# First mixing layer of a two-layer FNet and GeGLU kernel: hidden-side products of the last 1024 rows as seven turned block products

## The chip, the cores and the metric

One NeuronCore of a Trainium2 chip runs the whole program. The metric is device time in microseconds (us) of one execution. Engines are called as the profile calls them: PE is TensorE, DVE VectorE, ACT ScalarE, POOL GpSimd, SP SyncE, which issues most loads. Each engine works through its own list of instructions in the order in which the list was written when the program was built; a helper (`schedule_with_timeline_sim`) fixes these lists at build time.

## The reference

The input x has 2048 rows of 512. Two kinds of layer alternate, and the pair is applied twice (layers 0 to 3 in the kernel):

```python
def _A_ref(x, dft_seq_re, dft_seq_im, dft_hid_re, dft_hid_im):
    a = jnp.einsum("bsd,ed->bse", x, dft_hid_re)
    b = jnp.einsum("bsd,ed->bse", x, dft_hid_im)
    y = jnp.einsum("ts,bse->bte", dft_seq_re, a) - jnp.einsum("ts,bse->bte", dft_seq_im, b)
    return y
def _B_ref(x, w_gate, w_up, w_down):
    return (_gelu(x @ w_gate) * (x @ w_up)) @ w_down
x = x + _A_ref(_layernorm(x, axis=-1), ...)
x = x + _B_ref(_layernorm(x, axis=-1), ...)
```

## The kernel before

**Precision.** Each fp32 operand is divided into two fp32r parts, hi and lo (`split`: ACT writes hi at L157, DVE writes lo = src - hi at L159). Each product is three matmuls of 128x512, hi by hi, hi by lo, lo by hi (`mm3`, L214 to L216).

**A mixing layer** (`mix`, layers 0 and 2) forms the sequence-side product first, for four blocks b = 0 to 3 of 512 output rows, then multiplies its two results (real m = 0, imaginary m = 1) by the hidden-side matrices `wh`. The sequence side of a block is a 2x2 block product done with seven products (Winograd's form): A11 and A12 products, made for all four blocks at the beginning of the layer (`FORE`), then the stage "S2" (products S2, S1, S3 in a skewed order; for each of 8 pieces three DVE sums, `make_s2`, and three splits) and the stage "S4" (products S4 and A22). So S2 has 144 matmuls and S4 has 96. At the end of S4, DVE reads the PSUM banks (`plus`, L194) to finish the four columns pieces `cs[m, c]` of the block.

**The hidden side** of a block is done in one of two ways.

- Plain (`hid_groups`): eight pieces (m, c), each split and multiplied on four row tiles: 8 x 4 x 3 = 96 matmuls, in the order of `EARLY_HID` (2 pieces, between S2 and S4), `MID_HID` (4) and `LATE_HID` (2). The rows of x are put into the PSUM banks first (`seed`, L208), and ACT copies the finished banks out (`x_out`, L201).
- Paired (`pair_groups`, with `PAIRED = {2: (2, 3)}`: layer 2, blocks 2 and 3 together): the 1024 rows are again a 2x2 block product in seven products P1 to P7, each of 4 pieces k on 2 banks, 7 x 4 x 2 x 3 = 168 matmuls. The result comes out turned (columns on partitions), so that DVE transposes it in 32x32 blocks and adds it to x (`turned_into`, L815 and L197), and x is loaded and stored in that form (`pair_wide_load`, `pair_out`). DVE also makes differences of the pieces (`arrived`, `pair_sums`). In the first block of a pair P1 and P2 are used (2 pieces early, 6 late), in the second P7 and P4 (2 early, 6 late); P6, P5 and P3 (`PAIR_REST`, 12 products of 6 matmuls) run beside the first window of the next layer through the list `spare` (`beside_mix`).

The paired form needs other pieces of the hidden-side weights: `whd[k]`, seven pieces for each of 4 values of k, made from `whc` by `weight_steps(k, whc, whd)`: three loads, four sums on half tiles, four splits, seven stores to DRAM on POOL's queue. They are made in layer 1, second window (w = 1), through `spare`.

**What sets the order.** `take` works ahead: up to 7 items (`AHEAD`) are loaded and split before they are used. Between hidden-side products jobs called chores are run, `-(-len(chores) // hid_left)` after each (`chores_at`): from block 1 on they are the norms, transposes, sums and splits of the next layer's first operand (`block_steps`), and in layer 0 two weights of that layer's up projection (`wgu`, from `weight_steps`). `down_pieces` puts the making of down-projection weights beside layer 0 as well.

**A feed-forward layer** (`geglu`, layers 1 and 3) has two windows w of 1024 rows and goes over 14 steps n in each. In layer 1, w = 0, it also makes the remaining weights, and it starts (`first(0)`) with a product whose bank is copied by ACT as seed of the next one (L208).

Of the kernel before, what the change touches and what calls it, by code (L numbers as in the profile page):

```python
# [53 lines left out]
def fnet_geglu(ctx: ExitStack, tc: tile.TileContext, x_in, ws, wh, wgu, wdn, wdc, whc, out):  # L54
# [410 lines left out]
    PAIR_REST = [(name, k) for name in ("P6", "P5", "P3") for k in (2, 3, 0, 1)]  # L465

    def pair_items(names):
        return [(F32R, (piece(whd[k], FORM[name]),), make_pair(name, k), (name, k)) for name, k in names]

    def skewed(n):  # L470

# [6 lines left out]
    def plan(layer):  # L478

        fore, steps = FORE[layer], []  # L480
        steps += [(b, "A11") for b in range(fore)] + [(b, "A12") for b in range(fore)]
        for b in range(NB):
            if b >= fore:
                steps += [(b, "A11"), (b, "A12")]
            if b in PAIRED.get(layer, ()):
                n = PAIRED[layer].index(b)
                steps += [(b, "S2"), (b, PAIR_EARLY[n]), (b, "S4"), (b, PAIR_LATE[n])]
            else:
                steps += [(b, "S2"), (b, EARLY_HID), (b, "S4"), (b, MID_HID), (b, LATE_HID)]
        return steps  # L490
# [23 lines left out]
    def mix_items(layer):  # L514
        def raw(make, *tiles):
            items.append((F32, tiles, make, None))

        for b, what in plan(layer):
            tiles = [[ws[(b * 2 + m) * NS + k] for k in range(NS)] for m in range(2)]
            (a11, a12), (a21, a22) = ((r[:NK], r[NK:]) for r in tiles)  # L520
            hold = b >= FORE[layer]
            if what == "A11":
                for k in range(NK):
                    raw(as_is if bare(layer, b, what, k) else make_a11(k) if hold else plain, a11[k])
            elif what == "A12":
                for k in range(NK):
                    raw(plain, a12[k])
            elif what == "S2":
                for i, k in skewed(3):
                    if layer and (b, k) in wss:  # L530
                        raw(plain, wss[b, k][i])
                    elif i == 0:
                        raw(make_s2(layer, b, k), a21[k], a22[k], *(() if hold else (a11[k],)))
                    else:
                        raw(make_s1(k) if i == 1 else make_s3(k))
            elif what == "S4":
                for i, k in skewed(2):
# [6 lines left out]
            elif b in PAIRED.get(layer, ()):  # L544
# [277 lines left out]
    def mix(layer):  # L822
        hid, sums, chores, hid_left = {}, {}, [], [0]

        def chores_at(b):
            if b == NB - 3:
                norms, others = block_steps(layer + 1, 0)
                later.update(norms=norms[NT:], fetches=others[:ND], others=others[ND:])
                return norms[:NT]
# [38 lines left out]
        xu, xv, pair_banks, kept_p, pair_wide, late_v, sums_due = {}, {}, {}, {}, {}, {}, []  # L868

        def arrived(b, m, c):  # L870
            if b not in paired:
                return
            t = cs.pop((m, c))
            if b == paired[0]:
                (xv if m else xu)[c] = t
                cs["P2" if m else "P1", c] = t
                return
# [20 lines left out]
        def pair_wide_load(n):  # L898
# [3 lines left out]
            moved(pair_wide[n], xs[layer, paired[n]], lambda v, rows: nc.sync.dma_start(v, rows))  # L902

        def pair_out(n):
            moved(pair_wide[n], xs[layer + 1, paired[n]], lambda v, rows: nc.gpsimd.dma_start(rows, v))

        LAST = {"P1": 3, "P2": 1, "P7": 3, "P4": 1, "P6": 1, "P5": 1, "P3": 1}
        FIRST = {"P1": 0, "P2": 2, "P7": 0, "P4": 2}
# [48 lines left out]
            pair_product(*PAIR_REST[i])  # L957

        def pair_groups(b, groups):
            n, early = paired.index(b), groups in PAIR_EARLY  # L960
            if early:
                chores.extend(chores_at(b))
                hid_left[0] = 16 if n else 8
                if not n:
                    fetch_sums(paired[1])
                pair_wide_load(n)
            for i, (name, k) in enumerate(groups):
                if not early and not n and i == 2:
                    s2_seeded(paired[1])
# [7 lines left out]
            if n and not early:  # L977
                pair_banks["P6"] = [ps8.get() for _ in range(2)]
                for c in range(2):
                    seed(pair_banks["P6"][c], kept_p["P1"][c])  # L980
                spare.extend(lambda i=i: pair_rest(i) for i in range(len(PAIR_REST)))

        def down_pieces(b, at):
            for _ in range(DOWN_RUNS[at][b]):
# [52 lines left out]
        def a12(b):  # L1037
            stream["more"] = 0
            if layer and b == 0:
                lend("x")  # L1040
                lend("z")
            side = side_banks.pop(b)
            for k in range(NK):
                six(side, "B21", k, False, k == NK - 1, "21" if b == NB - 1 else None)
# [14 lines left out]

        def s2(b):  # L1060
            last = b == NB - 1
            if b == 0:
                lend("z")
                lend("x")
            cs.update(cs_next)
# [36 lines left out]

        def s4(b):
            last = b == NB - 1
            if b == NB - 4:
                sb.reclaim("z")
            if paired and b == paired[0] - 1:
                sb.reclaim("x")
            one, three = sides.pop(b)
            u = us.pop(b)  # L1110
# [158 lines left out]
    def geglu(w, layer):  # L1269
# [517 lines left out]
```

## Time and profile before

| what | value |
|---|---|
| median of 3 runs | 1596.6 us (1596.59 to 1599.89) |
| span of the profiled execution | 1596.4 us |
| its instructions | 22835 |
| mean granted TensorE clock | 1.000 |
| bytes by DMA | 431.75 MB, mean 270 GB/s |
| chain that ended last, PE's share | 91% |

In the rows of groups, the columns are line, engine, operation, tiles written and read, shape and count, then after the bar busy time in us, mean ns of one instruction, and after the next bar the idle time ahead of them with what ended it. In the rows by stage the columns are the stretch in us, its length, and for each engine busy time and in brackets the number of instructions that touch the stretch, then the granted clock, the share of DMA time and GB/s. In the rows in order of time the columns are start in us, length in us, engine, line, operation, tiles, count, and in square brackets the idle time ahead with what ended it.

### The profile page before, as it was taken

Reading aid. Unit: us, or ns where it says so; the run is one execution under the profiler, and the core shown is the slowest. Engines: PE = TensorE matmul, PEld = TensorE weight load, DVE = VectorE, ACT = ScalarE, POOL = GpSimd, SP = SyncE. Lnnn points to the kernel's source line nnn. Section 1 sums busy time; section 2 is a strip of 40 time slices with the busy share of each in tenths; the row PEclk is TensorE's granted clock in tenths of the full one; section 3 lists DMA queues with packets and bytes.
Section 4 is the critical chain, followed back from the end, with each engine's and each line's share of the span. In section 5 each row is a group of like instructions: output and inputs, shape, how many; then the busy total and the mean of one; then the engine's idle time right before and its main releaser. Section 6 shows DMA issues by size and latency. Waiting matters only on the chain.

```text
span 1596.4 us, 22835 instructions
## 1 busy us (share of the span) xinstructions
PE 1590.0 (100%) x6984; PEld 1311.2 (82%) x6984; DVE 1169.2 (73%) x2030; ACT 891.6 (56%) x1731; POOL 294.9 (18%) x505
## 2 busy tenths in 40 slices
PE   9999999999999999999999999999999999999999
PEld 6888888888888888888888888888888888888887
DVE  7997878888689794665879767778895557844574
ACT  8955465755777553666657535556553565333460
POOL 4122111251456101330040000101301000000000
PEclk9999999999999999999999999999999999999999
DMA  9898888996988999997895876878978958895445
GB/s 352 289 336 310 292 319 274 359 315 201 324 317 321 285 319 295 332 363 239 288 303 177 272 248 215 272 239 256 254 258 275 284 182 253 300 291 175 133 145 158
DMA packets 244058, 431.75 MB, mean 270 GB/s; under 512 B 29344, under 2 KB 68512, under 8 KB 242912
## 3 DMA queue, kind: packets, MB, share of 16 engines
q1 hardware_dynamic: 214128, 337.21, 66.2%
q0 software_dynamic: 27120, 90.99, 15.7%
q10 hardware_dynamic: 2688, 2.10, 0.5%
q8 instruction: 55, 0.90, 0.2%
q14 instruction: 67, 0.55, 0.1%
HBM read 341.31 MB, written 88.87 MB: 269 GB/s over the span
## 4 chain that ended last, share of the span: by engine, by line
PE 91%; issue 3%; DMA 3%; DVE 2%; ACT 1%; POOL 1%; SPq 0%; DVEq 0%; POOLq 0%; ACTq 0%
PE p L214 30%; PE p L215 30%; PE p L216 30%; DVE s L159 1%; DMA s<-ws 1%; DMA s<-t 1%; PE p L1010 0%; ACT s L157 0%; DMA s<-x 0%; DVE s L190 0%; POOL rstd L628 0%; DMA wide<-ws 0%; POOL s L754 0%; DVE xwide L190 0%; POOL wb L323 0%
## 5 line engine op out<-in xcount | busy, mean ns | idle before, releaser
L215 PE MATMUL p<-s,s 128*128 128x512 f32 x2312 | 897.4, 389 | 0.8 <-DVE s L159 0.8
L216 PE MATMUL p<-s,s 128*128 128x512 f32 x2312 | 891.8, 389 | 0.0
L214 PE MATMUL p<-s,s 128*128 128x512 f32 x2312 | 860.4, 389 | 0.3 <-ACT p L208 0.2
L157 ACT ACTIVATE s<-s 128x512 fp32r<-128x512 f32 (+1 forms) x855 | 481.3, 608 | 265.3 <-DVE s L190 73.6
L159 DVE TENSOR_TENSOR s<-s,s 128x512 fp32r<-128x512 f32 (+1 forms) x855 | 536.6, 661 | 115.3 <-ACT s L157 97.7
L215 PEld LDWEIGHTS p<-s,s 128*128 128x128 f32 x2312 | 433.9, 188 | 91.9 <-DVE s L159 1.9
L214 PEld LDWEIGHTS p<-s,s 128*128 128x128 f32 x2312 | 433.9, 188 | 91.7 <-ACT p L208 0.9
L216 PEld LDWEIGHTS p<-s,s 128*128 128x128 f32 x2312 | 434.0, 188 | 90.3
L194 DVE TENSOR_TENSOR s<-s,p 128x512 f32<-128x512 f32 x201 | 135.6, 682 | 160.3 <-PE p L216 138.1
L190 DVE TENSOR_TENSOR s<-s,s 128x512 f32<-128x512 f32 (+1 forms) x413 | 243.5, 609 | 6.2 <-DMA s<-ws 2.8
L201 ACT ACTIVATE s<-p 128x512 f32<-128x512 f32 x232 | 134.3, 593 | 108.0 <-PE p L216 106.3
L1264 ACT ACTIVATE s<-s 128x512 f32<-128x512 f32 x84 | 52.8, 628 | 46.4 <-DVE s L194 45.5
L628 POOL TENSOR_SCALAR rstd<-rstd 128x1 f32<-128x1 f32 x40 | 19.6, 489 | 237.2 <-ACT s L627 229.3
L1264 ACT ACTIVATE s<-p 128x512 f32<-128x512 f32 x28 | 16.7, 598 | 83.2 <-PE p L216 81.6
L323 POOL DMA_DIRECT2D wb<-s x84 | 46.1, 550 | 92.7 <-ACT s L157 70.5
L159 DVE TENSOR_TENSOR s<-xwide,s 128x512 fp32r<-128x512 f32 (+1 forms) x52 | 34.9, 679 | 29.2 <-ACT s L157 29.2
L651 ACT ACTIVATE s<-s,shift,rstd 128x512 f32<-128x512 f32 x59 | 47.5, 812 | 15.2 <-DVE shift L618 8.5
L1280 DVE TENSOR_TENSOR s<-s,p 128x512 f32<-128x512 f32 x56 | 38.2, 683 | 23.7 <-PE p L216 23.7
L197 DVE TENSOR_TENSOR s<-s,s 128x512 f32<-128x512 f32 (+1 forms) x71 | 42.8, 609 | 11.9 <-DMA s<-ws 10.4
L208 ACT ACTIVATE p<-p 128x512 f32<-128x512 f32 x56 | 32.6, 585 | 24.0 <-PE p L216 23.7
L157 ACT ACTIVATE s<-xwide 128x512 fp32r<-128x512 f32 (+1 forms) x52 | 31.6, 622 | 25.5 <-DVE xwide L194 18.2
L1201 POOL DMA_DIRECT2D wc<-s x42 | 30.5, 728 | 70.8 <-ACT s L157 61.9
(104 smaller groups left out, 614.9 us busy)
## 6 DMA issues: line engine op xcount, KB each, us to landing
s<-ws SPq DMA_DIRECT2D x404, 256.0 KB, 5.2
s<-wb SPq DMA_DIRECT2D x294, 256.0 KB, 5.2
s<-wc SPq DMA_DIRECT2D x182, 256.0 KB, 4.7
wb<-s POOLq DMA_DIRECT2D x98, 256.0 KB, 4.9
s<-wh SPq DMA_DIRECT2D x84, 256.0 KB, 5.3
s<-x SPq DMA_DIRECT2D x55, 256.0 KB, 5.4
wc<-s POOLq DMA_DIRECT2D x49, 256.0 KB, 5.3
xwide<-ws SPq DMA_DIRECT2D x37, 256.0 KB, 5.3
```

The source lines that it names most:

```text
L157: newest["ACT"] = nc.scalar.activation(hi, src, AF.Copy)
L159: newest["DVE"] = nc.vector.tensor_tensor(lo, src, f32(hi), op=ALU.subtract)
L190: nc.vector.tensor_tensor(out, a, b, op=ALU.subtract)
L194: bank_read["DVE"] = nc.vector.tensor_tensor(out, a, b, op=ALU.add)
L197: nc.vector.tensor_tensor(out, a, b, op=ALU.add)
L201: bank_read["ACT"] = nc.scalar.activation(v, src, AF.Copy)
L214: nc.tensor.matmul(ps, ah, bh, start=start, stop=False, skip_group_check=True)
L215: nc.tensor.matmul(ps, ah, bl, start=False, stop=False, skip_group_check=True)
L216: newest["PE"] = nc.tensor.matmul(ps, al, bh, start=False, stop=stop, skip_group_check=True)
L323: nc.gpsimd.dma_start(a, f32(t))
L651: nc.scalar.activation(z, x, AF.Identity, bias=shift, scale=rstd)
L1264: nc.scalar.activation(t, g, AF.Gelu_apprx_tanh)
```

## The change

`PAIRED` now holds layer 0 too. Blocks 2 and 3 of layer 0 go the paired way; their `P6`, `P5` and `P3` products run beside steps n = 0 and 1 of layer 1, w = 0 (`beside_mix` starts there at n = 0). The pieces `whd` are made as chores of blocks 0 and 1 of layer 0, two values of k in each, ahead of the chores that were there, and no longer in layer 1, w = 1. Norms of the next layer's rows that were spread over eight products of 12 matmuls in block 2 are now spread over eight products of 6. A path for a pair that isn't the last one is added too, and is not used by this table. The core of the diff:

```diff
-PAIRED = {2: (2, 3)}
-LATER = 3
+PAIRED = {0: ((2, 3),), 2: ((2, 3),)}
+LATER = 4
...
-            if b in PAIRED.get(layer, ()):
-                n = PAIRED[layer].index(b)
+            if paired_with(layer, b):
+                n = paired_with(layer, b).index(b)
                 steps += [(b, "S2"), (b, PAIR_EARLY[n]), (b, "S4"), (b, PAIR_LATE[n])]
...
         def chores_at(b):
+            jobs = []
+            if layer == 0 and paired and b < ND // 2:
+                two = [weight_steps(k, whc, whd) for k in range(2 * b, 2 * b + 2)]
+                jobs = [two[0][0]] + [run for i, (_, runs) in enumerate(two) for run in [load for load, _ in two[i + 1:]] + runs]
+            return jobs + next_layer(b)
+
+        def next_layer(b):
...
-        paired = PAIRED.get(layer, ())
...
+        paired = {b for p in PAIRED.get(layer, ()) for b in p}
+        first_paired = min(paired, default=NB)
+        by_pair = {b: p for p in PAIRED.get(layer, ()) for b in p}
...
         def beside_mix(n):
-            run = spare.pop(0) if spare and (layer > 1 or n >= 1) else None
+            run = spare.pop(0) if spare and (w == 0 or n >= 1) else None
...
         if layer == 1 and w and PAIRED:
-            jobs = [weight_steps(k, whc, whd) for k in range(ND)]
+            jobs = [] if 0 in PAIRED else [weight_steps(k, whc, whd) for k in range(ND)]
```

In all, PE's list goes from 6951 rows to 6927, DVE's from 2030 to 2082, ACT's from 1658 to 1662. Two places of these lists are spoken of in the prediction. In their rows a tile's number tells it from the others; `p` is a PSUM bank, `s` a slot of SBUF.

**Place 1** is DVE's list in layer 0 from the end of S4 of block 2 (the read of the bank that S4 closes last) to the lo parts of the first S1 pieces of block 3's stage S2. Before, from the read of `p1_3102` to `s51_3783`, the lo part of the first S1 piece, 25 rows, 4 of them on half tiles:

```order
L194 TENSOR_TENSOR s26_3363<-s26_3363,p1_3102 128x512
L194 TENSOR_TENSOR s88_3365<-s88_3365,p2_3103 128x512
L197 TENSOR_TENSOR s20_3719<-xwide_1457,s20_3719 128x512
L197 TENSOR_TENSOR s22_3729<-s62_3727,s22_3729 128x512
L197 TENSOR_TENSOR s48_3461<-s27_3462,s48_3461 128x256
L190 TENSOR_TENSOR s68_3460<-s79_3459,s27_3462 128x256
L185 SCALAR_TENSOR_TENSOR s15_3766<-s26_3363,s85_3765 128x512
...
L159 TENSOR_TENSOR s51_3783<-s90_3721,s40_3782 128x512
```

Now, from the read of `p1_3233` to `s41_3967`, the lo part of the third S1 piece, 39 rows, 4 of them on half tiles; the first S1 piece's is the 28th of them:

```order
L194 TENSOR_TENSOR s31_3488<-s31_3488,p1_3233 128x512
L745 STREAM_TRANSPOSE wide_3648<-s55_3912 128x16x32
L194 TENSOR_TENSOR s79_3490<-s79_3490,p2_3234 128x512
L197 TENSOR_TENSOR s85_3838<-s17_3836,s85_3838 128x512
L159 TENSOR_TENSOR s90_3853<-s24_3834,s35_3852 128x512
L197 TENSOR_TENSOR s3_3848<-s22_3846,s3_3848 128x512
L197 TENSOR_TENSOR s72_3591<-s18_3592,s72_3591 128x256
L190 TENSOR_TENSOR s89_3590<-s34_3589,s18_3592 128x256
...
L190 TENSOR_TENSOR s48_4045<-s74_2957,s37_3566 128x512
L190 TENSOR_TENSOR s51_4047<-s26_2959,s69_3568 128x512
...
L159 TENSOR_TENSOR s41_3967<-s91_3886,s88_3966 128x512
```

On PE's list there were 85 matmuls between the last one into `p1_3102` and the first that reads `s51_3783`; there are now 49 between the last into `p1_3233` and the first that reads the first S1 piece, and 69 up to the first that reads `s41_3967`. The 39 rows hold, besides S2's sums and splits, the sums (half tiles) and three of the splits of an up-projection weight, two transposes of the next layer's norms, and the two differences of `arrived` (`s48_4045`, `s51_4047`).

**Place 2** is ACT's list at the start of layer 1, around the copy of the first bank into the next one (L208). Before, it comes after four copies of finished banks (L201) and one half-tile split:

```order
L201 ACTIVATE xwide_1457<-p5_4068 128x512
L626 ACTIVATE mean_4996<-total_4995 128x1
L201 ACTIVATE xwide_1457<-p6_4070 128x512
L627 ACTIVATE s54_4992,rstd_4993<-s11_4824,mean_4996 128x512
L201 ACTIVATE xwide_1457<-p7_4242 128x512
L201 ACTIVATE s50_4749<-p0_4244 128x512
L157 ACTIVATE s71_4739<-xwide_1457 128x256
L208 ACTIVATE p2_4768<-p1_4761 128x512
```

Now it comes after splits of pieces of P7, P4 and P6 (and of one operand of layer 1), the last of which, of `s24_3834`, waits for a sum of `pair_sums`:

```order
L157 ACTIVATE s70_4652<-s85_4641 128x512
L157 ACTIVATE s30_4662<-s18_4497 128x512
L183 ACTIVATE s82_4700<-s57_4327 128x512
L157 ACTIVATE s36_4646<-s6_4638 128x512
L183 ACTIVATE s78_4694<-s65_4325 128x512
L157 ACTIVATE s46_4736<-s24_3834 128x512
L208 ACTIVATE p4_4814<-p3_4807 128x512
```

On DVE's list the row that writes that `s24_3834` is the 21st from the one that reads `p2_4050`, the bank that the S4 product of block 3 closes (3 of the 21 are on half tiles); on PE's list 40 matmuls stand between the last into `p2_4050` and the one that needs the copy `p4_4814`.

More of the change, by code (lines that the diff above doesn't have):

```diff
@@ L464, in fnet_geglu, with paired_with @@
     )
-    PAIR_REST = [(name, k) for name in ("P6", "P5", "P3") for k in (2, 3, 0, 1)]
+    PAIR_REST = tuple((name, k) for name in ("P6", "P5", "P3") for k in (2, 3, 0, 1))
     def pair_items(names):
         return [(F32R, (piece(whd[k], FORM[name]),), make_pair(name, k), (name, k)) for name, k in names]
+    def paired_with(layer, b):
+        return next((p for p in PAIRED.get(layer, ()) if b in p), ())
     def skewed(n):
@@ L873, in arrived @@
             t = cs.pop((m, c))
-            if b == paired[0]:
+            if b == by_pair[b][0]:
                 (xv if m else xu)[c] = t
@@ L959, in pair_groups @@
         def pair_groups(b, groups):
-            n, early = paired.index(b), groups in PAIR_EARLY
+            pair_now[0] = by_pair[b]
+            n, early = by_pair[b].index(b), groups in PAIR_EARLY
+            if groups is PAIR_REST:
+                for i in range(len(groups)):
+                    pair_rest(i)
+                    step()
+                    for _ in range(-(-len(chores) // hid_left[0]) if chores else 0):
+                        chores.pop(0)()
+                    hid_left[0] -= 1
+                return
             if early:
                 chores.extend(chores_at(b))
[L963 to L966, printed above, removed]
+                hid_left[0] = 16 if n and b == NB - 1 else 20 if n else 8
+                if b + 1 < NB:
+                    fetch_sums(b + 1)
+                pair_wide_load(b, n)
             for i, (name, k) in enumerate(groups):
-                if not early and not n and i == 2:
-                    s2_seeded(paired[1])
+                if not early and b + 1 < NB and i == (4 if n else 2):
+                    s2_seeded(b + 1)
                 pair_product(name, k)
@@ L980, in pair_groups @@
                     seed(pair_banks["P6"][c], kept_p["P1"][c])
-                spare.extend(lambda i=i: pair_rest(i) for i in range(len(PAIR_REST)))
+                if b == NB - 1:
+                    spare.extend(lambda i=i: pair_rest(i) for i in range(len(PAIR_REST)))
         def down_pieces(b, at):
@@ L1041, in a12 @@
                 lend("z")
+            if layer and first_paired == 0 and b == FORE[layer] - 1:
+                sb.reclaim("x")
+                sb.reclaim("z")
             side = side_banks.pop(b)
@@ L1061, in s2 @@
             last = b == NB - 1
-            if b == 0:
+            if b == 0 and first_paired:
                 lend("z")
@@ L1104, in s4 @@
             last = b == NB - 1
-            if b == NB - 4:
+            if b == NB - 4 and first_paired:
                 sb.reclaim("z")
-            if paired and b == paired[0] - 1:
+            if b == first_paired - 1:
                 sb.reclaim("x")
```

16 lines of the change are left out of this document (9 added, 7 removed).

## The prediction

> **What bounds the kernel now.** I read the page first, then PE's waits, then the order of time at one crowded place.
>
> ```profile
> span 1596.4 us, 22835 instructions
> ...
> PE 1590.0 (100%) x6984; PEld 1311.2 (82%) x6984; DVE 1169.2 (73%) x2030; ACT 891.6 (56%) x1731; POOL 294.9 (18%) x505
> ```
> ```profile
> PE p L1693 <- POOL ident masks.py:199: 1.4, 1, 1.4
> PE p L215 <- DVE s L159: 0.8, 1, 0.8
> PE p L214 <- ACT p L208: 0.2, 1, 0.2
> ```
>
> PE waits for other engines 2.4 us in all, 1.4 of it before the first matmul. So PE sets the time, and each matmul taken away saves its start-to-start time, as long as no engine makes PE wait in its place. That time is read from 27 rows in order of time, first and last:
>
> ```profile
> 1098.83 0.39 PE L214 MATMUL p<-s,s 128*128 128x512 f32 x1
> ...
> 1104.72 0.39 PE L216 MATMUL p<-s,s 128*128 128x512 f32 x1
> ```
>
> 5.89 us over 26 steps: 0.2265 us a matmul. (Its own length, 0.39, overlaps the next.) DVE at the same place of layer 2, where block 2 of the pair ends and block 3 begins:
>
> ```profile
> 1099.03 1.37 DVE L194 TENSOR_TENSOR s<-s,p 128x512 f32<-128x512 f32 x2 [0.21 <-PE p L216]
> ...
> 1102.12 0.69 DVE L197 TENSOR_TENSOR s<-s,s 128x512 f32<-128x512 f32 x1
> 1102.72 0.69 DVE L159 TENSOR_TENSOR s<-s,s 128x512 fp32r<-128x512 f32 x1
> ...
> 1105.13 0.69 DVE L185 SCALAR_TENSOR_TENSOR s<-s,s 128x512 fp32r<-128x512 f32 x1
> ```
>
> Two things are to be seen. The read of a bank (L194) begins when PE has closed it, and all that stands behind it on DVE's list waits too. From there DVE goes back to back: from 1102.12 to 1105.13 five instructions, 0.602 us each. A half tile takes less, an ACT split and a copy of a bank as follows, busy time by count:
>
> ```profile
> L190 DVE TENSOR_TENSOR s<-s,s 128x256 f32<-128x256 f32 x116 | 46.8, 417 | 0.2
> ```
> ```profile
> L157 ACT ACTIVATE s<-s 128x512 fp32r<-128x512 f32 (+1 forms) x855 | 481.3, 608 | 265.3 <-DVE s L190 73.6
> ...
> L208 ACT ACTIVATE p<-p 128x512 f32<-128x512 f32 x56 | 32.6, 585 | 24.0 <-PE p L216 23.7
> ```
>
> So 0.40, 0.56 and 0.58 us. By block of layer 0 (block 0 to block 3, about 76 us each, the third row a little long):
>
> ```profile
> 95.00:171.00 76.00, 76.00 (x337) 62.94 (x336) 65.08 (x112) 39.56 (x72) 15.71 (x27) 1.00 0.88 320
> 171.00:247.00 76.00, 76.00 (x337) 62.94 (x336) 59.26 (x100) 44.31 (x93) 15.40 (x24) 1.00 0.82 282
> 247.00:329.00 82.00, 82.00 (x364) 67.89 (x363) 69.11 (x119) 53.76 (x109) 19.74 (x34) 1.00 0.95 337
> 329.00:405.00 76.00, 76.00 (x337) 62.94 (x336) 58.65 (x100) 39.87 (x76) 27.09 (x41) 1.00 0.78 233
> ```
>
> DVE (the third pair of numbers) is at 77 to 86% there, PE at 100%.
>
> **The change part by part.**
>
> *Matmuls.* Plain, blocks 2 and 3 take 2 x 96 = 192 hidden-side matmuls; paired they take 168. 24 less at 0.2265 us: **5.4 us saved**. 72 of the 168 move into layer 1, so layer 0 is 96 matmuls or 21.7 us shorter, 48 in each of its two last blocks.
>
> *DVE's work.* It grows by 52 instructions: 12 more splits (28 for 16), 16 for `arrived` and `pair_sums`, 8 adds from banks, 16 for turning. And what it already did in blocks 2 and 3 (S2, S4, norms, weights) stays, beside 10.9 us less of PE in each: DVE's busy share of block 3, 58.65 of 76, becomes 58.65 of 65 ahead of anything added. What matters is where this work stands in DVE's list between a bank that PE closes and a part that PE needs. I counted both in the two lists, and a wait is the difference.
>
> *Place 1, start of block 3's S2.* Before, 25 rows up to the first S1 piece (21 at 0.602 and 4 at 0.40: 14.2 us) against 85 matmuls (19.3 us): 5 us to spare, because 72 hidden-side matmuls of block 2, MID and LATE, ran in between with only 6 splits. Now 36 matmuls run there. 39 rows stand before the third S1 piece: 35 x 0.602 + 4 x 0.40 = 22.7 us, against 69 x 0.2265 = 15.6 us. **PE waits 7.0 us** here. It isn't less: DVE cannot begin earlier than the closing of the bank. It is more if a row waits for its hi part, a transpose for its norm or a sum for its load.
>
> *Place 2, end of block 3.* From the read of `p2_4050` 21 rows (18 x 0.602 + 3 x 0.40 = 12.0 us) to the sum that P6 starts from, then ACT's split and copy (0.56 + 0.58): 13.2 us. PE has 40 matmuls meanwhile, 9.1 us. **PE waits 4.1 us**; all four reads of S4's last banks are inside these rows, so nothing starts earlier. Behind the waiting L208 on ACT stand the copies of layer 1's banks; PE is stopped anyway. The former wait for L208, 0.2 us, goes into this one.
>
> *P6, P5, P3 in layer 1.* DVE has 67 rows there, from the first use of P4's bank to a split that is needed 185 matmuls later: at most 67 x 0.602 = 40.3 us for 41.9 us. Taken as 0; if a row in it waits, up to some 4 us. The nearest stretch, where layer 3 runs the same products without making weights, has DVE nearly full and PE losing little:
>
> ```profile
> 1160.00:1200.00 40.00, 39.78 (x175) 32.47 (x174) 39.05 (x66) 21.90 (x39) 0.00 (x0) 1.00 0.78 259
> ```
>
> *The pieces of wh, made beside blocks 0 and 1.* Each of four weights costs DVE 5 half tiles and 3 whole ones, 3.8 us, so 7.6 us a block: 65.08 + 7.6 = 72.7 and 59.26 + 7.6 = 66.9 of 76. Cost 0, hidden by DVE's idle time; in the closest place in the list there, 3 whole and 2 half rows stand against 10 matmuls, 0.3 us. Their 28 stores go to POOL's queue, priced by those of the down weights:
>
> ```profile
> L1201 POOL DMA_DIRECT2D wc<-s x42 | 30.5, 728 | 70.8 <-ACT s L157 61.9
> ```
>
> 14 x 0.73 = 10.2 us a block on top of POOL's 15.71 and 15.40 of 76. Behind a store that waits for its split stand the norms' rstd, for which ACT waits; from block 2 on the wh stores are done, so I take 0, up to 1 us. Their 12 loads stand ahead of loads of ws on SP's queue, and what they cost is a rival below. In layer 1, w = 1, the same work goes away where PE didn't wait: 0. The 0.8 us wait is at the start of layer 2, behind loads of ws; I leave it, +-0.8.
>
> *Sum:* -5.4 + 7.0 + 4.1 = +5.7 us on the span of 1596.4, so 1602.1. The median of the runs is 0.2 above that span: **1602.3 us**.
>
> **The rivals.**
>
> *Loads come late in blocks 0 to 2.* The transfers that come in, and the closest waits:
>
> ```profile
> wq<-s POOLq DMA_DIRECT2D x28, 256.0 KB, 5.7
> ...
> s<-whc SPq DMA_DIRECT2D x8, 128.0 KB, 4.9
> s<-whc SPq DMA_DIRECT2D x4, 256.0 KB, 7.6
> ```
> ```profile
> GB/s 352 289 336 310 292 319 274 359 315 201 324 317 321 285 319 295 332 363 239 288 303 177 272 248 215 272 239 256 254 258 275 284 182 253 300 291 175 133 145 158
> ```
> ```profile
> DVE s L197 <- DMA s<-ws: 4.3, 3, 2.6
> ...
> ACT s L157 <- DMA s<-ws: 4.1, 1, 4.1
> ```
>
> That is 28 x 0.262 + 8 x 0.131 + 4 x 0.262 = 9.4 MB on top of 45.7 (320 and 282 GB/s for 76 us each): 55.1 MB in 152 us, 363 GB/s, as much as the best fortieth of the span. If no more than 337 (block 2's row) is sustained, they take 163.5 us, 11.5 too long: 1602.3 + 11.5 = 1613.8. Against it: loads are asked for seven items ahead, and in these blocks (95 to 250 us) late loads of ws held DVE and ACT up by only 8.4 us and PE not at all. It decides once the lead is used up. The Trainium skill (DMA: Bandwidth & Descriptors, the table at its head) gives about 358 GB/s as the limit of HBM for one core; by it the 55.1 MB would be only 2 us late, an estimate. The trace disagrees with it as a hard limit, by the slice of 363.
>
> *The clock drops in a wait.* The granted clock is 1.00 in every row shown, but no wait in them is longer than 1.4 us. If after place 2 half the clock were granted for as long as the wait, 4.1 us, PE would lose 2.1 us: 1604.4. The Trainium skill (TensorE: Matmul & The Clock Gate, Part 1) says that an idle window of about 3.4 us halves the clock until PE has been busy for as long; no run here shows that yet.
>
> *Only one place bites,* because some rows of the other finish ahead: with place 1 alone 1596.6 - 5.4 + 7.0 = 1598.2, no change.
>
> *The gain is kept:* PE waits at neither place, 1596.6 - 5.4 = 1591.2, faster. The mechanism would be that DVE does place 1's 39 rows beside the 69 matmuls, and the point where that decides is 15.6 / 39 = 0.40 us a row. For it: PE hasn't waited for DVE but for 0.8 us, though DVE was full in stretches. Against it: 0.602 in the rows above.
>
> **How the numbers follow.** Forecast 0.62, late loads 0.14, clock 0.05, one place 0.11, gain kept 0.08. A difference under 0.2% (3.2 us) cannot be told from none here. Faster 0.08; same 0.11 (one place); slower 0.81. The range goes down to 1598, where one place alone ends, and up to 1611, which takes in most of the late loads (8.7 of 11.5 us) and the small unknowns (waits for hi parts, 4 us in layer 1, 0.8). Left out: the gain kept, and what is beyond 1611.
>
> **What would show it.** In the profile after: 24 matmuls less; layer 0 ending about 10 to 11 us earlier, not 22; PE waits of about 7 us in all for DVE's L159 or ACT's L157 near 310 to 330 us, spread over several S2 pieces, and of about 4 us for ACT's L157 and L208 near 385; DVE without idle time in both. It would be wrong if PE's waits stay under 3 us, if DVE is seen idle in them (then loads or POOL's norms hold it), or if the waits lie ahead of 250 us (then the loads).

## The result, and the profile after

| | median of the runs, us | range | ratio to before, 95% interval |
|---|---|---|---|
| before, beside the change | 1597.3 | 1596.6 to 1599.9 (4 runs) | |
| the change | 1647.4 | 1641.3 to 1651.5 (4 runs) | 1.0304 [1.0272, 1.0335] |
| forecast | 1602.3 | 1598 to 1611 | |

The change makes the kernel 50 us slower. The forecast had the sign and not the size. The runs of the change lie 10 us apart, those of before 3. The profiled execution of the change, at the lower end of its runs, shows on its page:

```profile
span 1639.4 us, 22801 instructions
...
PE 1598.6 (98%) x6960; PEld 1308.1 (80%) x6960; DVE 1200.3 (73%) x2082; ACT 894.8 (55%) x1735; POOL 291.1 (18%) x505
```

PE has the 24 matmuls less and DVE the 52 instructions more that were counted, and DVE's share of the span is 73% as before. What is new stands in PE's waits (total us, times, longest):

```profile
PE p L215 <- DVE s L159: 10.5, 9, 4.3
PE p L214 <- DVE s L194: 7.8, 1, 7.8
PE p L214 <- ACT p L208: 5.3, 3, 4.6
PE p L214 <- ACT s L157: 3.4, 5, 1.3
PE p L214 <- DMA s<-wq: 2.8, 2, 1.7
PE p L214 <- DMA s<-wc: 2.4, 1, 2.4
PE p L214 <- ACT s L201: 2.0, 3, 1.0
```

Before, three such rows summed to 2.4 us. Now all rows together make 36.6 us, for DVE, ACT and DMA alike; those of 2 us and more are shown. By stage (block 0, block 1, block 2, block 3 with the start of layer 1; PE is the first engine, DVE the third, the granted clock the first number behind the engines):

```profile
95.00:172.00 77.00, 77.00 (x341) 63.76 (x340) 63.18 (x112) 41.50 (x75) 23.38 (x39) 1.00 0.87 313
172.00:254.00 82.00, 77.90 (x336) 62.09 (x335) 68.89 (x121) 42.07 (x78) 20.06 (x31) 1.00 0.91 330
254.00:332.00 78.00, 70.86 (x299) 54.76 (x297) 62.52 (x107) 53.06 (x120) 22.81 (x34) 1.00 0.94 313
332.00:415.00 83.00, 68.63 (x279) 54.80 (x279) 74.20 (x126) 39.72 (x70) 22.47 (x41) 0.92 0.73 211
```

PE loses nothing in block 0, some 4 us in block 1, 7 in block 2 and 14 in block 3, where DVE is busy 74 of 83 us and the clock falls to 0.92. PE's busy time hides a part of the loss, since a matmul at half clock counts as busy. So I add up, over the start times of PE's matmuls, what each step takes beyond 0.2267 us, from block 1 on, for this kernel and for those told below. The columns are places in PE's order; the "end of block 3" column holds P4 to the first products of layer 1, and P6, P5 and P3 where a run has them there. The last two columns part at PE's 2100th matmul, which still lies in the first window of layer 1 (at 526.0 us in the change).

| run | block 1 | S2 of block 2 | rest of block 2 | S2 of block 3 | S4 of block 3 | end of block 3 | layer 1 up to matmul 2100 | behind | sum |
|---|---|---|---|---|---|---|---|---|---|
| before | 0 | 0 | 0 | 0 | 0 | 0.4 | 0 | 1.7 | 2.0 |
| the change | 6.3 | 4.0 | 5.0 | 11.8 | 0 | 9.7 | 7.1 | 7.5 | 51.3 |
| e1_no_making | 0 | 1.1 | 0 | 10.9 | 0 | 3.0 | 8.1 | 15.8 | 38.9 |
| e2_making_only | 5.9 | 4.9 | 1.0 | 0 | 0 | 0.4 | 0 | 2.2 | 14.5 |
| e3_later_norms | 5.3 | 7.6 | 4.8 | 11.1 | 0 | 9.9 | 0 | 24.0 | 62.7 |
| e4_no_up_making | 6.9 | 5.3 | 4.6 | 6.3 | 7.0 | 4.7 | 6.5 | 11.0 | 52.3 |
| e5_slots_held | 0 | 0 | 0 | 6.1 | 0 | 0.2 | 0 | 1.2 | 7.5 |
| e6_slots_freed | 6.0 | 4.5 | 4.7 | 9.2 | 0 | 0.2 | 4.5 | 11.2 | 40.2 |
| e7_making_no_rows | 0 | 0 | 4.3 | 0 | 0 | 0.2 | 0 | 1.6 | 6.0 |
| e8_no_making_freed | 0 | 1.6 | 0 | 6.3 | 0 | 1.2 | 7.6 | 11.8 | 28.5 |
| e9_rest_in_layer0 | 6.6 | 5.1 | 4.7 | 12.3 | 0 | 8.2 | 11.2 | 3.6 | 51.8 |
| e10_wide_on_pool | 5.7 | 4.4 | 8.0 | 8.8 | 0 | 10.0 | 7.1 | 14.6 | 58.5 |
| e11_all_three | 0 | 1.7 | 0 | 4.5 | 0 | 7.2 | 18.7 | 3.0 | 35.1 |
| e12_all_and_delay | 0 | 0 | 0 | 7.0 | 0 | 6.7 | 2.9 | 9.4 | 25.9 |
| e13_rows_on_sp | 0 | 8.0 | 0 | 2.5 | 0 | 6.7 | 13.7 | 6.2 | 37.0 |
| e14_rest_and_delay | 7.0 | 7.8 | 4.9 | 11.3 | 0 | 8.1 | 1.6 | 3.1 | 43.9 |

For the change, 51.3 less the 2.0 of before and the 5.4 saved is 43.9; the two spans differ by 43.0. So this table holds the whole difference between the two profiled executions; the median run of the change is 6 us longer than its profiled one. It is one execution for each run: single entries move by some us, as four runs with the same S2 of block 3 and free slots show (2.5, 4.5, 6.3, 7.0). And no run is the change with rows simply taken out: the helper orders the lists of each kernel anew. At place 2, for example, DVE has 20 rows from the read of `p2_4050` to the read that the first matmul of layer 1 needs; in e1_no_making there are 12.

### The profile page after: what moved, and what is told of

It reads as the page before. It is cut to its first block, busy times and chain, and to the rows that moved or that the text cites. A ratio compares the mean times of both kernels' runs of the same rounds, so it can differ in the third digit from the quotient of the medians.

```text
span 1639.4 us, 22801 instructions
## 1 busy us (share of the span) xinstructions
PE 1598.6 (98%) x6960; PEld 1308.1 (80%) x6960; DVE 1200.3 (73%) x2082; ACT 894.8 (55%) x1735; POOL 291.1 (18%) x505
## 4 chain that ended last, share of the span: by engine, by line
PE 81%; DMA 6%; DVE 5%; issue 3%; POOL 2%; ACT 1%; SPq 1%; DVEq 0%; POOLq 0%; ACTq 0%
PE p L215 27%; PE p L214 27%; PE p L216 27%; DVE s L159 2%; DMA s<-ws 2%; DVE s L190 1%; DMA s<-t 1%; DMA wc<-s 1%; ACT s L157 1%; DMA s<-wc 1%; SPq L251 1%; POOL s L759 1%; PE p L1034 1%; DMA xwide<-wdc 1%; DVE s L194 1%
## 5 line engine op out<-in xcount | busy, mean ns | idle before, releaser
L157 ACT ACTIVATE s<-s 128x512 fp32r<-128x512 f32 (+1 forms) x886 | 496.8, 608 | 295.4 <-DVE s L190 78.3
L159 DVE TENSOR_TENSOR s<-s,s 128x512 fp32r<-128x512 f32 (+1 forms) x886 | 556.3, 663 | 129.3 <-ACT s L157 112.7
L190 DVE TENSOR_TENSOR s<-s,s 128x512 f32<-128x512 f32 (+1 forms) x440 | 263.2, 618 | 19.6 <-DMA s<-ws 13.4
L194 DVE TENSOR_TENSOR s<-s,p 128x512 f32<-128x512 f32 x214 | 144.3, 683 | 170.3 <-PE p L216 140.0
L201 ACT ACTIVATE s<-p 128x512 f32<-128x512 f32 x236 | 136.3, 593 | 115.0 <-PE p L216 105.5
L1291 ACT ACTIVATE s<-s 128x512 f32<-128x512 f32 x84 | 52.8, 629 | 49.3 <-DVE s L194 49.0
L633 POOL TENSOR_SCALAR rstd<-rstd 128x1 f32<-128x1 f32 x40 | 14.4, 361 | 297.0 <-ACT s L632 296.2
L1307 DVE TENSOR_TENSOR s<-s,p 128x512 f32<-128x512 f32 x56 | 38.3, 683 | 26.7 <-PE p L216 26.4
L197 DVE TENSOR_TENSOR s<-s,s 128x512 f32<-128x512 f32 (+1 forms) x79 | 48.2, 618 | 6.2 <-DMA s<-ws 5.5
L208 ACT ACTIVATE p<-p 128x512 f32<-128x512 f32 x56 | 32.6, 584 | 24.1 <-PE p L216 21.8
L745 DVE STREAM_TRANSPOSE wide<-s 128x512 f32<-128x512 f32 x32 | 22.7, 708 | 25.6 <-ACT s L656 25.6
L630 ACT ACTIVATE s<-s 128x512 f32<-128x512 f32 x39 | 24.3, 623 | 30.9 <-DMA s<-x 15.5
L759 POOL DMA_DIRECT2D s<-t x64 | 35.0, 552 | 26.0 <-PE p L216 11.4
```

What stands on the lines that cost most here:

```text
L157: newest["ACT"] = nc.scalar.activation(hi, src, AF.Copy)
L159: newest["DVE"] = nc.vector.tensor_tensor(lo, src, f32(hi), op=ALU.subtract)
L190: nc.vector.tensor_tensor(out, a, b, op=ALU.subtract)
L194: bank_read["DVE"] = nc.vector.tensor_tensor(out, a, b, op=ALU.add)
L197: nc.vector.tensor_tensor(out, a, b, op=ALU.add)
L201: bank_read["ACT"] = nc.scalar.activation(v, src, AF.Copy)
```

## The experiments

My theory after the first look at the traces had four parts: the making of wh's pieces is not free, the rows of the turned products make PE wait at the two places forecast, loads come late in blocks 2 and 3, and the rows of x reach layer 1 late.

**Two halves of the change.** First the turned products alone, reading stored halves in place of the pieces, with the making left in layer 1 (the products' values are other ones):

```diff
+    return whs[i, k][:, ...] if raw else piece(whd[k], FORM[name])
...
-            if layer == 0 and paired and b < ND // 2:
+            if False:
...
-            jobs = [] if 0 in PAIRED else [weight_steps(...)]
+            jobs = [weight_steps(...)]
```

> Layer 0 keeps the paired products, but their weights are read as pieces of wh that the plain blocks have stored anyway (so the output is not the reference's), and the seven pieces for layer 2 are made in layer 1, second window, as before the change. So DVE, ACT, POOL and SP lose the making beside blocks 0 and 1, the paired products stay. If the making is what takes DVE's slack and the later waits are its backlog, nearly all of the 50 us of waits go: 1595 to 1608 us. If the paired products' own rows are what PE waits for, only the 14 us lost ahead of block 2's end (320 us) go: 1630 to 1637 us.

Then the making alone, with the plain products in layer 0:

```diff
-PAIRED = {0: ((2, 3),), 2: ((2, 3),)}
-LATER = 4
+PAIRED = {2: ((2, 3),)}
+LATER = 3
...
-            if layer == 0 and paired and b < ND // 2:
+            if layer == 0 and b < ND // 2:
...
```

> The reverse: layer 0 plain as before the change, and only the making of the seven pieces moved beside blocks 0 and 1. If the making alone costs PE what was lost ahead of block 2's end, 6 us in block 0 and 4 us in block 1: 1603 to 1611 us. If plain blocks give DVE enough slack to hide it: 1596 to 1599 us.

Measured: 1631.7 us, ratio 1.0212 [1.0196, 1.0228], and 1610.3 us, 1.0079 [1.0064, 1.0094]. The making costs 12 us by itself, the turned products 33, and both 50, more than their sum. The table says where: the making costs 5.9 us in block 1, 3.5 of them in its S2, and 4.9 us in S2 of block 2. Of the 5.0 us in the rest of block 2 neither half alone shows more than 1.0.

**Why the making isn't hidden.** In the change DVE waits once in block 0 for a load of a down weight, whose sums stand in its list:

```profile
155.89 0.42 DVE L197 TENSOR_TENSOR xwide<-s,xwide 128x256 f32<-128x256 f32 x1 [3.72 <-DMA xwide<-wdc]
```

and from then on it has no idle time to catch up with. The same 40 us (160 to 200) in before, and in the run with the making alone:

```profile
160.00:200.00 40.00, 40.00 (x178) 33.10 (x178) 34.31 (x58) 19.64 (x37) 6.99 (x11) 1.00 0.83 292
```
```profile
160.00:200.00 40.00, 37.69 (x162) 29.91 (x161) 39.57 (x69) 23.83 (x44) 15.10 (x23) 1.00 1.01 384
```

DVE (third pair) goes from 34.31 to 39.57 of 40 us, that is, it is full, and PE loses 2.3. This run takes DVE's rows of the making out and keeps its loads, its stores and four ACT copies for each weight, in place of the four high parts (it leaves out wh's sums and low parts):

```diff
         def sums():
+            if place is whd:
+                return
...
+                if place is whd:
+                    t = sb.get(F32R)
+                    nc.scalar.activation(t, src[0], AF.Copy)
+                    nc.gpsimd.dma_start(to[:, :512], f32(t))
```

> The plain products in layer 0 and the making of wh's pieces beside blocks 0 and 1, as in the run that moved only the making (1610.3 us), but without the making's rows on DVE (no sums, no low parts): its loads, its 28 stores and one ACT copy for each stay. Theory that DVE's rows are the price (DVE has no slack left in block 0 once it has waited for one load): 1597 to 1601 us. Rival (the loads and stores delay the stream, or the slots that the making holds): 1606 to 1612 us.

Measured: 1602.0 us, 1.0021 [1.0010, 1.0031]. 8 of the 12 us go, and all of the 10.8 in block 1 and in S2 of block 2; DVE has its slack again. (The run also holds one tile where the making holds a high and a low part, so it frees some slots too; the two are not told apart.)

```profile
160.00:200.00 40.00, 40.00 (x178) 33.13 (x177) 34.12 (x56) 22.93 (x42) 10.09 (x18) 1.00 0.97 349
```

The 4 us that stay are two short waits in block 2, with a stretch at half clock behind them; the loads and stores were not taken away apart, so whether they cause these is open. The same two waits stand at the same matmuls in the change (1.5 and 1.0 us), so they are no mark of the turned products. 1602.0 is a little above the range of the theory.

**The norms' place, and the up weights' rows.** Two runs on the later places: the norms of layer 1's second window begin later (`LATER = 6` for 4), and the two up-projection weights are not made beside blocks 2 and 3 (their pieces are loaded at the same points, with other data).

> The full change, with LATER = 6 instead of 4: the norms of layer 1's second window begin 14 steps (two up-projection steps, some 20 us) later. In the profile after, ACT stands at such a norm for 7.7 us at 470 us because the rows of blocks 2 and 3 come out late, and PE waits 4.6 us for a copy behind it, then runs 11 matmuls at half clock, 7.1 us in all. If that is the order of ACT's list against late rows, the 7 us go: 1635 to 1642 us. If something else (POOL's stores, the loads) holds layer 1 there, no change: 1644 to 1650 us.

> The full change, with the two up-projection weights of layer 0's chores not made: their pieces are read from stored down-projection pieces (so the output is not the reference's). DVE loses 5 half and 3 whole rows twice in blocks 2 and 3, 7.6 us, POOL 14 stores. If PE's waits at places 1 and 2 are DVE's list being too long there, place 1 loses 3 to 4 us of its 8 and with it the half clock behind it, place 2 some: 1632 to 1641 us. If they come from late loads, 1643 to 1650 us.

Measured: 1650.4 us (1.0329 [1.0314, 1.0344]) and 1644.7 us (1.0297 [1.0280, 1.0314]). Neither helps. The first takes the 7.1 us in layer 1 away and loses 24.0 behind it in place of 7.5: the wait moved. In the second, block 3 loses 18.0 us (its three columns) in place of 21.5, now partly in S4: taking DVE's rows for these weights out moves the loss more than it lowers it.

**Free slots.** The kernel's tiles of 128x512 come from 98 slots in SBUF, handed out in turn; a load can only be issued when the last user of its slot is done. Counting the free ones in the order in which the program is written (smallest, mean):

| | S4 of block 2 | S2 of block 3 | S4 of block 3 |
|---|---|---|---|
| before | 17, 21.8 | 15, 23.7 | 23, 32.2 |
| the change | 10, 14.0 | 1, 6.6 | 5, 15.0 |
| e4_no_up_making | 18, 22.2 | 5, 10.6 | 9, 19.1 |
| e5_slots_held | 7, 11.8 | 5, 13.7 | 13, 22.2 |
| e6_slots_freed | 18, 22.2 | 12, 17.6 | 16, 27.7 |

The turned products hold tiles that the plain ones don't: pieces of two blocks, four products copied out of PSUM, and the wide tile that before was lent out as four more slots. In the trace of the change DVE then waits for sums' operands in S2 of block 3 (320 to 372 us), which before it never did there. All three waits end behind the forecast's place 1, at 347, 362 and 368 us:

```profile
DVE s L190 <- DMA s<-ws: 8.4, 3, 4.6
```

Three runs test this: before with ten slots taken out of use, the change with the up weights' pieces neither made nor held in blocks 2 and 3 but loaded at the end of layer 0, and the latter without the making of wh's pieces.

```diff
+            if layer == 0 and (b, what) == (2, "S2"):
+                held_back.extend(sb.get() for _ in range(10))
```
```diff
-                weights = [weight_steps(n) for n in range(2)] if layer == 0 else []
+                weights = []
-                if layer:
-                    weight_load(0)
-                    weight_load(1)
+                weight_load(0)
+                weight_load(1)
```

> The kernel before, with ten of its 98 SBUF slots taken out of use from block 2's S2 to the end of layer 0; nothing else is changed. Theory of the slots (the paired products and the weights made beside them leave so few free slots that a load can only be issued when a slot falls free, and the rows that need the loads come late): in the trace the loads of ws wait on the SP queue for slots, DVE waits for DMA in blocks 2 and 3, and PE loses 8 to 25 us there: 1606 to 1624 us. Rival (the paired products lose by their own rows on DVE and ACT, slots have nothing to do with it): 1597 to 1602 us.

> The full change, but the first two weights of the up-projection are neither made nor held in blocks 2 and 3: 14 pieces are loaded at the end of layer 0, as layer 2 does it (the data are those of the down-projection; it leaves out the making of two weights). By the count of slots in the program's order the free ones in blocks 2 and 3 are 12 to 16 at least in place of 1 to 5. Against the run that left out only the making and kept the slots full (1644.7 us): theory of the slots: the 16 us or so that PE lost in blocks 2 and 3 go for the most part, 1622 to 1634 us. Rival (the paired products' own rows, or the wide load that stands in SP's queue): 1640 to 1648 us.

> The turned products in layer 0 with no making at all beside layer 0: wh's operands are stored halves (1631.7 us with the up-projection's two weights made), and those two weights are loaded at the end of layer 0 as in the run with the freed slots. Theory of the slots: what PE lost at the start of block 3's S2 and at the start of layer 1 (some 14 us) goes, and the wait for rows in layer 1 (8 us) and the ones behind it stay: 1612 to 1621 us. Rival (the turned products' own rows): 1626 to 1634 us.

Measured: 1602.8 us (1.0038 [1.0024, 1.0052]), 1637.3 us (1.0243 [1.0214, 1.0272]), 1616.6 us (1.0130 [1.0092, 1.0167]). The first and the second lie between the ranges of theory and rival, the third in the theory's, but by its number: the loss at the start of block 3's S2 was to go, and 6.3 of the 10.9 us stay. So slots have a price by themselves, 6.1 us in S2 of block 3, but a smaller one than I expected; the ten held slots also left more free in that stage (5 at least, 13.7 on average) than the change does (1 and 6.6). Freed in the change, they bring 7 us against the run with the same rows of DVE (intervals apart): the end of block 3 loses 0.2 us in place of 4.7, S2 and S4 of block 3 lose 9.2 in place of 13.3. That run also takes 14 loads off SP's queue in these blocks, so the gain is not the slots' alone for certain. And DVE's waits for loads of ws in S2 of block 3 shrink but don't end: 11.6 us in the run with the same rows and full slots, 6.0 with slots freed, 4.9 without the making too. Without the making, PE still waits at S2 of block 3, for a low part of a sum:

```profile
PE p L215 <- DVE s L159: 3.3, 1, 3.3
```

That is the forecast's place 1, and it is there without the making and with slots to spare, though DVE has also waited 2.2 us for loads of ws in the rows ahead of it.

**Loads behind a blocked queue.** In the change the wide loads of x stand on SP's queue ahead of loads of ws. Moved to POOL's queue (in both mixing layers, since the line serves both):

```diff
-... lambda v, rows: nc.sync.dma_start(v, rows))
+... lambda v, rows: nc.gpsimd.dma_start(v, rows))
```

> The full change, but the loads of the wide tiles of x (four for each paired block) are issued on POOL's queue in place of SP's; the second of them stands for 7 us in SP's queue, ahead of the loads of ws, until the turned rows have left the tile. Theory of the blocked queue (the loads of ws at the start of block 3's S2 are late by that wait): 5 to 10 us of the 11.6 that PE loses there go: 1637 to 1643 us. Rival (DVE's rows and the full slots hold that place, the queue would wait for a slot anyway): 1645 to 1652 us.

Measured: 1645.4 us (1.0288 [1.0256, 1.0320]), the rival's range. S2 of block 3 loses 8.8 in place of 11.8, the rest of block 2 8.0 in place of 5.0: no gain.

**Late rows.** The rows of x of blocks 2 and 3 are stored when P3 and P5 have ended, in layer 1. In the change's trace, first POOL's store, then SP's load of mixed rows, then ACT's norm of them:

```profile
458.53 2.60 POOL L919 DMA_DIRECT2D x<-xwide  x4
```
```profile
469.22 10.41 SPq L251 DMA_DIRECT2D s<-x  x16
```
```profile
477.56 0.63 ACT L630 ACTIVATE s<-s 128x512 f32<-128x512 f32 x1 [7.65 <-DMA s<-x]
```

ACT stands 7.65 us at the norm (L630), and the seed (L208) that PE waits 4.6 us for is behind it in ACT's list. The first trial moves P6, P5 and P3 to the end of block 3, in the full change; the second does so with the other two costs away too:

```diff
-                if n and b < NB - 1:
+                if n and (b < NB - 1 or layer == 0):
                     steps.append((b, PAIR_REST))
...
```

> The full change, but layer 0's last twelve products (P6, P5 and P3, 72 matmuls) run at the end of block 3 and no longer beside layer 1's first matmuls; no work is added or left out. Theory of the late rows (blocks 2 and 3's rows of x are only stored when P3 and P5 have ended, some 70 us into layer 1, so the norms of layer 1's second window, its turned tiles and the loads behind them come late): PE's waits at the later part of layer 1 and the two behind them (7.1, 2.3 and 3.5 us) go, and with the slots that free up sooner most of the 9.7 us at the start of layer 1: 1624 to 1637 us. Rival (those waits come from DVE's and ACT's rows and move to the end of block 3): 1642 to 1652 us.

> The turned products in layer 0 with three of the suspected costs taken away together: no making of wh's pieces beside layer 0 (stored halves are read), the first two weights of the up-projection not made in blocks 2 and 3 but loaded at the end of layer 0, and P6, P5 and P3 at the end of block 3. It leaves out the making of two weights. If the three theories (DVE's rows of the making, the slots, the late rows) hold the whole loss but for the start of block 3's S2, 6 us stay there and 5.4 are saved: 1596 to 1606 us. Rival (the turned products cost more in rows of their own than these places show): 1610 to 1620 us.

Measured: 1644.1 us (1.0283 [1.0268, 1.0298]) and 1625.5 us (1.0167 [1.0150, 1.0184]): both miss, the first on the rival's side and the second beyond it. But the edit did more than I had written. Where nothing is left beside layer 1, the kernel's test `if spare:` no longer delays the norms, so they stood in ACT's list ahead of their rows once more. ACT in the second run, 440 to 462 us:

```profile
ACT s L633 <- DMA s<-x: 11.9, 1, 11.9
```

The next runs put the delay back, without and with the making, and one of them stores layer 0's turned rows from SP's queue:

```diff
-            if spare:
+            if spare or layer == 1:
                 pace[0] = 7
```

> The run with the three costs taken away (1625.5 us), with the norms of layer 1's second window begun as late and paced as in the full change: with P6, P5 and P3 in layer 0 the kernel's own test for that delay no longer held, so the norms stood in ACT's order before their rows were stored, and PE lost 16 us in one place of layer 1. As there, the making of two weights is left out. Theory of the late rows (an ACT norm whose row of x is still on its way through POOL's queue holds up ACT's copy that PE waits for): those 16 us go, 1605 to 1613 us. Rival (the wait moves to a later step of layer 1): 1618 to 1626 us.

> The full change with nothing left out, P6, P5 and P3 at the end of block 3 (1644.1 us), and the norms of layer 1's second window begun and paced as in the full change. Theory of the late rows: the 8 us that PE loses in the later part of layer 1 and the 2 to 4 behind them go: 1630 to 1637 us, the best that a full version of this change has given, and slower than the kernel before by the making and by the start of block 3's S2. Rival (the wait moves): 1641 to 1648 us.

> The run before this in the list, with layer 0's eight stores of the turned rows issued on SP's queue in place of POOL's, where they stand among the stores of the up-projection's pieces. Theory that POOL's order of stores delays the rows: 2 to 6 us less than the run before this in the list. Rival (the rows are late because DVE's turned additions are, or the delay of the norms has already covered it): within 2 us of it, or slower where SP's queue stands still for DVE.

Measured: 1614.0 us (1.0091 [1.0069, 1.0114]), 1631.9 us (1.0212 [1.0197, 1.0228]), 1622.7 us (1.0158 [1.0137, 1.0179]). The first is 1 us above its range, the second inside. With the delay 11.5 and 12.2 us go, and in layer 1 up to matmul 2100 PE loses 2.9 for 18.7 and 1.6 for 11.2. In the first pair a part of it moves: behind that matmul PE loses 9.4 for 3.0, and 4.8 of the 9.4 still lie in the same window. In the first of these runs ACT no longer waits for x there, but for DVE:

```profile
ACT s L633 <- DVE s L1309: 4.7, 1, 4.7
```

So the late rows are shown as the cause of the longest waits in layer 1. Taking the stores off POOL's queue doesn't help: on SP's they cost 8.7 us more, and the loads behind them stand still for DVE (390 to 430 us):

```profile
SPq L337 <- DVE s L159: 16.5, 3, 8.3
```

The best full form of the change, 1631.9 us, stays 34 us behind the kernel before, so no version here beats it. What PE still waits for in it:

```profile
PE p L215 <- DVE s L159: 15.0, 10, 4.3
PE p L214 <- DMA s<-wq: 5.5, 1, 5.5
```

## Why the prediction was wrong

*The matmuls, -5.4:* right; 6984 became 6960, and the table closes with it.

*The pieces of wh, "Cost 0, hidden by DVE's idle time":* this step failed first, by 12 us. I compared DVE's work with the length of a block, 72.7 of 76 us. The work stands beside the hidden-side products of a block, and what it delays is S2 of the next, where DVE has three sums for each piece and little room. The average over a block said 3.3 us to spare; the 40 us that mattered had 0.4. A load that came 3.7 us late took a part of what there was; how much is not shown apart.

*Place 1, 7.0 us:* right in mechanism, and in the size of what was counted; what it left out is that DVE came late. PE's last matmul into `p1_3233`, the first that reads the first S1 piece, and the first that reads `s41_3967`:

```profile
319.20 0.39 PE L216 MATMUL p<-s,s 128*128 128x512 f32 x1
...
338.13 0.79 PE L215 MATMUL p<-s,s 128*128 128x512 f32 x1 [4.33 <-DVE s L159]
...
345.30 0.39 PE L215 MATMUL p<-s,s 128*128 128x512 f32 x1
```

DVE from the row ahead of its read of that bank to its next idle time:

```profile
321.59 0.69 DVE L159 TENSOR_TENSOR s<-s,s 128x512 fp32r<-128x512 f32 x1 [1.40 <-ACT s L157]
322.20 0.68 DVE L194 TENSOR_TENSOR s<-s,p 128x512 f32<-128x512 f32 x1
...
344.02 1.02 DVE L159 TENSOR_TENSOR s<-s,s 128x512 fp32r<-128x512 f32 x2
347.02 0.69 DVE L190 TENSOR_TENSOR s<-s,s 128x512 f32<-128x512 f32 x1 [1.98 <-DMA s<-ws]
```

The last of the three matmuls starts 26.1 us after the first; 70 steps of 0.2267 us are 15.9, so PE is 10.2 us late. Of these, 7.6 are there at the second one, and 2.6 come from matmuls at half clock behind its wait. DVE sets the pace: it goes through the 39 rows without a break, in 22.5 us for the forecast's 22.7, but starts on them 3.0 us after 319.20, held by a hi part just ahead. The forecast's 7.0 and these 3.0 make up the 10.2 within 0.2. The forecast's own words name such a case ("It is more if a row waits for its hi part"), without a price. The rest of this stage's loss are two waits of 1.1 and 0.8 us behind DVE's waits for ws. The four runs without the making and with slots to spare lose 2.5 to 7.0 us in this stage, but that 6.3 and 7.0 are so near the forecast is chance: without the up weights' rows, the forecast's sum over these kernels' own lists is 2.0 us (27 rows against 63 matmuls).

*Place 2, 4.1 us:* the stretch of DVE's list was right, the matmul that waits for it was not, and DVE came late here too. In the change PE stopped earlier, at the first matmul of layer 1, which writes a bank that DVE had still to read. That read is the 20th of the forecast's 21 rows, 11.4 us by its times, and only 30 matmuls, 6.8 us, stand against it in place of 40 and two rows of ACT: 4.6 us. And DVE, without a break in its order of time from 388 us on, began the first of these rows at 397.03, 3.6 us after the start of PE's last matmul into `p2_4050` (393.39). The first and the 20th row:

```profile
397.03 0.68 DVE L194 TENSOR_TENSOR s<-s,p 128x512 f32<-128x512 f32 x1
...
407.66 0.68 DVE L194 TENSOR_TENSOR s<-s,p 128x512 f32<-128x512 f32 x1
```

PE before, in and after the wait:

```profile
400.19 0.39 PE L216 MATMUL p<-s,s 128*128 128x512 f32 x1
408.39 0.80 PE L214 MATMUL p<-s,s 128*128 128x512 f32 x1 [7.81 <-DVE s L194]
408.99 0.63 PE L215 MATMUL p<-s,s 128*128 128x512 f32 x1
409.41 0.63 PE L216 MATMUL p<-s,s 128*128 128x512 f32 x1
...
413.05 0.40 PE L214 MATMUL p<-s,s 128*128 128x512 f32 x1
413.28 0.39 PE L215 MATMUL p<-s,s 128*128 128x512 f32 x1
```

With slots freed and the up weights' rows gone, 0.2 and 1.2 us are lost at the end of block 3; with these rows gone and slots short, 4.7. Which part of that is the slots and which the new order of the lists is open.

*P6, P5, P3 in layer 1, "Taken as 0; if a row in it waits, up to some 4 us":* wrong. I counted DVE's rows and didn't follow the rows of x from their store to the norms. In the two columns of layer 1 and behind, the change loses 7.1 and 7.5 us; with P6, P5 and P3 earlier and the delay kept it is 1.6 and 3.1.

*The rivals.* Late loads had 0.14 and 1613.8 us, for the transfer rate of blocks 0 to 2. Loads did come late. In block 2, where this rival looked, PE waits 2.8 us for the new pieces themselves (wq, 272 to 276 us; 5.5 us in the best full form); whether bandwidth or their place in SP's queue makes them late is open. In block 3 the stage of 332 to 415 us moves only 211 GB/s, and holding or freeing slots moves the loss. The prediction counted the slots nowhere. The clock had 0.05 as a matter of one place; in the change 26 matmuls run at half clock, 0.2 us each, 5.2 us behind three waits. The forecast added what each place costs when all before it is on time. That did not hold: DVE came 3.0 us late to the first row of place 1 and 3.6 us late to that of place 2.

## What to carry to other kernels

Work that is put beside a busy engine is paid in the next stretch where that engine has no slack, so compare it there, in windows of tens of us, and not with the mean over a stage. A wait that is counted as rows against matmuls also needs the time at which the engine reaches the first of these rows, and the nearest matmul that any of them holds up, the reuse of a bank included. With an edit that keeps more tiles alive, count the free buffers in the program's order; here ten slots less cost 6.1 us in one stage. Follow what a moved product stores as far as its first reader; here ACT waited 7.65 us for a row four steps behind the moved products (turned addition, store, load, norm).

## What the hardware showed

The clock. After the step of 8.2 us above (a wait of 7.81) six matmuls follow at 0.427 us, then 0.227 again. Over the traces of all sixteen kernels, of 35 steps in which PE stood still for 2.8 us or more, 34 were followed by 5 to 13 such matmuls; of 25 between 1.6 and 2.8 us, 10 were, some of them with a second wait close by, and single ones from 2.2 us on. The Trainium skill (TensorE: Matmul & The Clock Gate, Part 1) says that the clock halves after an idle window of about 3.4 us, counted in windows that run on their own. The size of the step agrees; that waits of 2.2 to 2.8 us are enough shows that a window of that length need not be idle throughout. In the clock records of these traces each stretch at half clock inside the span lasts 3.41 us or two to four times that.

Transfers. In the making-only run's 160 to 200 us the core moved 384 GB/s, for 40 us, with its DMA engines busy throughout (share 1.01). The Trainium skill (DMA: Bandwidth & Descriptors, the table at its head) gives about 358 as HBM's limit for one core, half of what a stack gives to two; the trace, with one core at work, is above it.
